# Activations that come turned: centring by an accumulating DMA in place of TensorE transposes

## The chip, the cores and the metric

The kernel runs on one core of a Trainium2 chip. The metric is the device time of one execution in microseconds (us). The engines are named as the profile names them: PE (TensorE, matrix products; PEld is its loading of weights), DVE (VectorE), ACT (ScalarE), POOL (GpSimd) and SP (SyncE). Each works through a queue of its own in order and waits on semaphores for the others. DMAs are issued from the queues of SP, ACT and POOL.

## The reference

The input x has 2048 rows (tokens) of 512 features. Its rows are normalised, and two mixers work on the result: a linear attention with softmax feature maps, and a gated MLP whose gate mixes along the tokens. Both outputs and x are added.

```
xn = (x - mean(x)) / sqrt(var(x) + 1e-5)          # per row
A: q, k, v = xn @ wqkv, in 32 heads of 16
   phi(t)  = [softmax(t @ w_phi), softmax(-(t @ w_phi))]
   o       = phi(q) (phi(k)^T v) / (phi(q) sum_s phi(k) + 1e-6);   A = o @ wo
B: z = gelu(xn @ w_in);  z1, z2 = the halves of z;  z2 = layernorm(z2)
   B = (z1 * (w_sp @ z2 + b_sp)) @ w_out
out = x + A + B
```

All in float32.

## The kernel before

**Tiles.** x is cut into NT = 16 tiles of 128 tokens. A matrix product contracts over the partitions, so each tile is needed turned: features in the partitions, tokens along the row. For precision, every float32 operand is split in two parts (a rounded one, `h`, and the remainder, `l`), and a product is made of three matmuls (`mm3`, lines 55 to 57). ACT rounds (`round_h`, line 47) and DVE takes the remainder (`rest_l`, line 51).

**The first stage** (the part that the change touches) goes over the tiles `s` and, in each, takes the keys' projection of tile s with its softmax features (`proj_k`, `softmax_pair`), prepares tile s + 2 (`centered`), projects queries (`proj_q`, which starts late and catches up), adds the tile's features to a running sum (`add_kv`, by an accumulating DMA of POOL into `zacc`, and at s = 3, 7, 11, 13 and 15 by matmuls into `kvps`), projects the values of tile s + 1 (`proj_v`) and one half of the MLP's input product (`z1_raw`).

**Preparing a tile** (`centered`): `stats` takes mean and variance on DVE (lines 260 and 261); POOL negates the mean (`neg_mean`, line 265) and computes 1/sqrt(var + eps) (`rstd_of`, lines 92 and 93), which is applied later as a scale of ACT; ACT adds the negative mean to the tile (`center`, line 269); PE turns it with four 128x128 transposes into PSUM (`transposed`, line 275, tile `pt`); and `split_x` rounds it (ACT) and takes the remainder (DVE), both reading PSUM, into the tile `xT[s]`, which the projections of this tile read. The loads of x are issued by SP four tiles ahead (`fetch`, line 179), into XB = 5 buffers.

**Buffers.** PSUM gives four buffers of the tag "mm" to the projections of keys, queries and values and to `pt`. In SBUF, 16 slots of the pool `xz` hold the turned tiles `xT`, which stay; until they are all taken, the slots hold staged weights and, from `spare`, the features `er` of the key tiles 2, 3, 4, 5, 8 and 9.

**Order.** The order on each engine comes from a planner, which runs a model of the whole program and takes at each point the instruction of the highest priority (program order) that is ready by its own costs. `tc.issue_after(i)` pins what the block issues on i's engine behind i; `keep` does the same for the first tiles, whose order is written out by hand. Semaphores and the release of buffers are put in by the framework.

**Later stages**: the other half of the MLP's input product (`zps` with `w2`), the token mixing (`g`, matmuls from 281 us to 493 us in the profile below), and the output products (`pout`).

The host passes `x_t` to the kernel in the version before too: for each tile, the features in the partitions, and in row p the values of features p, 128 + p, 256 + p and 384 + p for its 128 tokens. It is not read there.

Of the kernel before, what the change touches and what calls it, by code (L numbers as in the profile page):

```python
# [10 lines left out]
F32 = mybir.dt.float32  # L11
F32R = mybir.dt.float32r
AF = mybir.ActivationFunctionType
ALU = mybir.AluOpType
# [4 lines left out]
P = 128  # L19
S, D, H, DH, FH = 2048, 512, 32, 16, 688  # L20
NT = S // P
ND = D // P
FC = FH // 2
NG = 4
NF = 2 * D
# [3 lines left out]
BL = 32  # L29
EPS_LN = 1e-5  # L30
EPS_DEN = 1e-6
XB = 5
NP = NT // 2
HP, QP = P // 2, P // 4
FP = 3 * P
# [4 lines left out]
def mixer(ctx: ExitStack, tc: tile.TileContext, x, x_t, wv, wqkT, phi_bd, wo, w_in, wst, b_r, w_out, out):  # L40
    nc = tc.nc
    pe, act, dve, pool, sp = nc.tensor, nc.scalar, nc.vector, nc.gpsimd, nc.sync


    def round_h(eng, h, src):
        if eng is act:
            return act.activation(h, src, AF.Copy).ins  # L47
        return eng.tensor_copy(h, src).ins

    def rest_l(l, src, h, eng=None):  # L50
        return (eng or dve).tensor_tensor(l, src, h.bitcast(F32), op=ALU.subtract).ins  # L51
# [18 lines left out]
    def xz_tile(n, dt, name):  # L70
        return xz.tile([P, SL], dt, tag="xz", name=name)[:, :n]

    mid = ctx.enter_context(ExitStack())
    dram = ctx.enter_context(tc.tile_pool(name="dram", bufs=1, space=DRAM))
# [2 lines left out]
    u_d = dram.tile([NT, FU, P], F32, name="u_d")  # L77
    kvT_d = dram.tile([P, D], F32, name="kvT_d")
    zb_d = dram.tile([P, NF], F32, name="zb_d")

    ident = cst.tile([P, P], F32, name="ident")
    make_identity(nc, ident)
# [4 lines left out]
    r_x = cst.tile([P, NT], F32, name="r_x")  # L87

    def rstd_of(mv, r, stats=None):
        if stats is not None:  # L90
            dve.bn_aggr(mv, stats)
        pool.tensor_scalar_add(mv[:, 1:2], mv[:, 1:2], EPS_LN)
        pool.tensor_tensor(r, mv[:, 1:2], mhalf, op=ALU.pow)

    def heads(ap):
        return ap.rearrange("p (h d) -> p h d", d=DH)
# [8 lines left out]
    def bc(ap, n):  # L105
        return ap.unsqueeze(2).to_broadcast([P, n, DH])

    def softmax_pair(pl, src, tag, scale=1.0, ebufs=2, meanwhile=lambda: None, er=None):

        mm = pl.tile([P, 2, H], F32, tag=tag + "mm", bufs=1, name="mm")  # L110
        dve.tensor_reduce(mm[:, 0], heads(src), axis=AX.X, op=ALU.max)
        dve.tensor_reduce(mm[:, 1], heads(src), axis=AX.X, op=ALU.min)
        if er is None:
            er = pl.tile([P, NF + 2 * H], F32, tag=tag + "e", bufs=ebufs, name="e")
        e, r = er[:, :NF], er[:, NF:]
        e2 = e.rearrange("p (h a d) -> p h a d", a=2, d=DH)
        dve.tensor_tensor(e2[:, :, 0], heads(src), bc(mm[:, 0], H), op=ALU.subtract)
        dve.tensor_tensor(e2[:, :, 1], bc(mm[:, 1], H), heads(src), op=ALU.subtract)  # L118
        act.activation(e, e, AF.Exp, scale=scale)  # L119
        meanwhile()  # L120
        sm = pl.tile([P, 2 * H], F32, tag=tag + "sm", bufs=1, name="sm")
        dve.tensor_reduce(sm, heads(e), axis=AX.X, op=ALU.add)  # L122
        dve.reciprocal(r, sm)
        return er
# [34 lines left out]
    mask = w1_pool.tile([P, 2 * P], F32, name="mask")  # L159
# [3 lines left out]
        pool.affine_select(out=mv_, in_=mv_, compare_op=ALU.is_ge, fill=0.0, base=base,  # L163
                           pattern=[[-k * DH, P // DH], [0, 2 * DH]], channel_multiplier=k)
    pool.tensor_tensor(mask[:, :P], mask[:, :P], mask[:, P:], op=ALU.add)
    mask = mask[:, :P]
    ones = w1_pool.tile([P, P], F32, name="ones")
    pool.memset(ones, 1.0)
    zacc = w1_pool.tile([P, NF], F32, name="zacc")
# [2 lines left out]
    with ExitStack() as p0:  # L172
        res = p0.enter_context(left("p0res", 1))
        wk = p0.enter_context(left("p0wk", 2))
        ps = p0.enter_context(psum("p0ps", 4))

        def load_x(s):
            t = wk.tile([P, D], F32, tag="x", bufs=XB, name="xt")
            sp.dma_start(t, x[s * P:(s + 1) * P, :])
            return t  # L180
# [5 lines left out]
        def stage(name, dt=F32):  # L186
            return xz_tile(2 * FH, dt, name).rearrange("p (a b) -> p a b", a=2)
# [6 lines left out]
        bd_t = stage("bd")  # L194
# [50 lines left out]
        xt, v, rounded, ready = {}, {}, [], []  # L245

        def fetch(s):
            if s < NT:
                xt[s] = load_x(s)

        def split_x(src):
            t = xz_tile(2 * D, F32R, "xT").rearrange("p (a b) -> p a b", a=2)
            xT.append(t)
            src = src.rearrange("p a b -> p (a b)")
            rounded.append(round_h(act, t[:, 0], src))
            return rounded[-1], rest_l(t[:, 1], src, t[:, 0])

        def stats(s, keep=lambda **ins: None):
            st6 = wk.tile([P, 6], F32, tag="st6", name="st6")
            dve.bn_stats(st6, xt[s])  # L260
            keep(dve=dve.bn_aggr(mv_x[:, s], st6).ins)

        def neg_mean(s):
            nm = wk.tile([P, 1], F32, tag="nm", name="nm")
            pool.tensor_scalar_mul(nm, mv_x[:, s, 0:1], -1.0)
            return nm

        def center(s, nm):
            return act.activation(xt[s], xt[s], AF.Identity, bias=nm).ins

        def transposed(s):
            xs = xt.pop(s)
            pt = ps.tile([P, ND, P], F32, tag="mm", name="pt")
            for c in range(ND):
                ins = pe.transpose(pt[:, c], xs[:, c * P:(c + 1) * P], ident).ins
            return pt, ins

        def centered(s):
            stats(s)
            nm = neg_mean(s)  # L280
            rstd_of(mv_x[:, s], r_x[:, s:s + 1])
            with tc.issue_after(rounded[s - 2]):
                center(s, nm)
            split_x(transposed(s)[0])

        def keep_v(s, p):
            v[s] = wk.tile([P, D], F32, tag="v", bufs=4, name="v")
            return act.activation(v[s], p, AF.Copy, scale=r_x[:, s:s + 1]).ins
# [5 lines left out]
        spare = {}  # L294

        def proj_k(s):
            er = spare[s].rearrange("p a b -> p (a b)")[:, :NF + 2 * H] if s in spare else None
            return softmax_pair(wk, proj(s, wqk_h[:, 1], wqk_l[:, 1]), "k", r_x[:, s:s + 1], er=er)

        def proj_q(s):  # L300
# [28 lines left out]
        wkT_t = load_rows.raw  # L329
        fetch(2)  # L330
        wqT = load_rows(wqkT[:D])
        wqT_t = load_rows.raw
        fetch(3)
        w1r = [stage("w1row") for _ in range(2)]
# [43 lines left out]
        t = xz_tile(2 * D, F32R, "xT").rearrange("p (a b) -> p a b", a=2)  # L378
# [8 lines left out]
        for cs, pt in zip(halves, pts):  # L387
            src = pt.rearrange("p a b -> p (a b)")
# [8 lines left out]
        p = ps.tile([P, D], F32, tag="mm", name="proj")  # L397
        proj(0, wv_h, wv_l, p, (0, 1, 2))
        keep(pe=proj.last)
        pt = turned(1)  # L400
# [4 lines left out]
        p = ps.tile([P, D], F32, tag="mm", name="proj")  # L405
# [18 lines left out]
        p = ps.tile([P, D], F32, tag="mm", name="proj")  # L424
        proj(0, wqk_h[:, 1], wqk_l[:, 1], p, (0, 1))
        keep(pe=proj.last)
        pt = turned(2)
# [18 lines left out]
        split_x(turned(3))  # L446
        z1_raw(wk, za, 0, 2)
        keep(pe=zproj.last)
        spare.update(zip((2, 3, 4, 5, 8, 9), [bd_t] + wkT_t + wqT_t[:1] + w1r))
        n1, nq = 1, 0  # L450
        for s in range(NT):
            fetch(s + 4)
            er = ek[s] if s < len(ek) else proj_k(s)
            if 1 < s < NT - 2:
                centered(s + 2)
            while nq < (s - 2) * NT // (NT - 3):
                proj_q(nq)
                nq += 1
            add_kv(s, er)
            if s == 0:  # L460
                tiles = fold_tiles(((za, "z"), (ps, "mm")))
                keep(pe=fold(0, wqT, tiles))
                folded(0, tiles)
            elif s == 1:
                proj_v(3)
            elif 2 < s < NT - 1:
                proj_v(s + 1)
            while n1 < s * (NT - LAG) // (NT - 1):
                z1_raw(wk, za, n1, 2)
                n1 += 1  # L470
            if s == 3:
                queue.close()
# [33 lines left out]
    NQ = NT // QC  # L506
    NC = NP * NQ


    SEQ = [(i, q) for i in range(NP) for q in (range(NQ) if i < NP - 1 else (1, 2, 3, 0))]  # L510

# [40 lines left out]
    with ExitStack() as p1:  # L552
# [44 lines left out]
        for s in range(NE):  # L597
            et = load_q(s, tb.tile([P, QW], F32, name="et") if s else tmp1.tile([P, 4, D], F32, tag="zhl", name="et").rearrange("p a b -> p (a b)")[:, :QW])
            tmp = zw.tile([P, 4, FC], F32, tag="z2", bufs=2, name="qtmp").rearrange("p a b -> p (a b)")[:, :NF]
            e, _ = q_fin(et, tmp, zb)  # L600
# [57 lines left out]
    for s in range(NT):  # L658
        p = zproj((kv_ps_p, zc, zbp, za)[s % 4], s, w2, (0, 1) if s % 2 == 0 else (1, 0))
# [7 lines left out]
        for k, q in p:  # L667
            ins = act.activation(z[:, k], q, AF.Gelu_apprx_tanh, scale=r_x[:, s:s + 1]).ins
# [5 lines left out]
        mv = zw.tile([P, 2], F32, tag="mv", bufs=2, name="mv")  # L674
# [61 lines left out]
    def gate(i, cb, z, u, ut, after=None):  # L736
# [10 lines left out]
        def turn():  # L747
# [3 lines left out]
            for b in range(0, P, BL):  # L751
                (pool if i == NP - 2 else sp).dma_start(dst[:, :, b:b + BL], src[b:b + BL].rearrange("p (m b) -> p m b", b=BL))

# [49 lines left out]
    for n in range(NC):  # L803
        i = SEQ[n][0]
        if n % NQ == 1 and i < NP - 1:
            z = load_z1(i)
        products(n, g)
        if n % NQ == NQ - 1 and i < NP - 1:
            c = gt.tile([P, 2, FU], F32, tag="c", name="c")
# [5 lines left out]
        if n + 2 < NC:  # L815
            A[n + 2] = prep_a(n + 2, raw.pop(n + 2))
        if n % NQ == NQ - 1 and i < NP - 1:
            turn = gate(i, cb, z, c, z, prep_a.last)
# [12 lines left out]
        if n == NC - 2:  # L831
            es[0], es[1] = first_q(0), first_q(1)
            t = xz_tile((KF + 1) * P, F32R, "u1")
# [10 lines left out]
    wk = ctx.enter_context(left("cwk", 2))  # L844
# [125 lines left out]
    p, nxt = {}, dict(enumerate(uT))  # L970
# [61 lines left out]
```

## Time and profile before

| | before |
|---|---|
| median of 3 runs (lowest to highest) | 628.2 us (628.04 to 629.95) |
| the profiled execution | 627.78 us |
| its span, first to last instruction | 626.1 us |
| busy PE / DVE / ACT / POOL | 619.1 / 508.8 / 280.7 / 104.8 us |
| mean granted clock of PE | 0.999 |
| moved by DMA | 98.40 MB |

All rows of the prediction come from this one profiled execution. A row of the timeline has start, duration, engine, line of the kernel, operation, output and inputs, shape, and in brackets the idle time of the engine before it with what ended it. A row of groups has the line, engine and operation, the shape, the count, the busy time in all and the mean duration of one in ns, and behind the second bar the idle time before these instructions. Matmuls overlap, so the starts of matmuls say more than their durations. A row of DMA issues ends with the size of one and the median time in us from issue to landing. A row of waits has the total, the count and the longest.

### The profile page before, as it was taken

To read this page: it belongs to the slowest core of one execution; us is meant where nothing else is said; L and a number is where in the kernel's file an instruction comes from. 1 tells how busy PE (TensorE), PEld (TensorE's weight loads), DVE (VectorE), ACT (ScalarE), POOL (GpSimd) and SP (SyncE) were. 2 spreads that over 40 slices of the span, in tenths; PEclk is the share of its full clock that TensorE was granted. 3 is DMA by queue.
4 is the path that set the end of the run, shared out by engine and by line. 5 is a ranking of instruction groups with operands and counts; after the bars stand their busy time and mean duration, and the time that the engine had idled before them with its cause. 6 is when DMAs were issued, how large, how long until landed. Compare 5 with 4: busy or idle time off the path is not lost.

```text
span 626.1 us, 11429 instructions
## 1 busy us (share of the span) xinstructions
PE 619.1 (99%) x4406; PEld 565.3 (90%) x4406; DVE 508.8 (81%) x893; ACT 280.7 (45%) x446; POOL 104.8 (17%) x187
## 2 busy tenths in 40 slices
PE   8999999999999999999999999999999999999996
PEld 7888888888888999999999999999999877788775
DVE  5999998987988398989898897696978899989211
ACT  5653434443333367877434444243445433334331
POOL 4142122111011015442000000000000212211110
PEclk9999999999999999999999999999999999999999
DMA  9445465354336868001454845637367799984722
GB/s 313 164 109 144 121 156 155 88 143 136 104 93 173 274 234 285 2 2 35 147 115 147 193 96 153 136 119 175 88 174 232 224 297 330 320 249 97 180 34 51
DMA packets 87590, 98.40 MB, mean 157 GB/s; under 512 B 46560, under 2 KB 59616, under 8 KB 87296
## 3 DMA queue, kind: packets, MB, share of 16 engines
q1 hardware_dynamic: 75200, 58.12, 32.4%
q0 software_dynamic: 10032, 33.92, 20.7%
q10 hardware_dynamic: 2304, 5.64, 2.4%
q8 instruction: 34, 0.56, 0.4%
q14 instruction: 20, 0.16, 0.1%
HBM read 56.37 MB, written 30.54 MB: 139 GB/s over the span
## 4 chain that ended last, share of the span: by engine, by line
PE 98%; DVE 0%; ACT 0%; POOL 0%; issue 0%; DVEq 0%; POOLq 0%
PE g L57 11%; PE g L56 11%; PE g L55 11%; PE proj L57 7%; PE proj L55 7%; PE proj L56 7%; PE zps L57 6%; PE zps L55 6%; PE zps L56 6%; PE pout L55 5%; PE pout L57 5%; PE pout L56 5%; PE ptq L890 1%; PE po L905 1%; PE kvps L319 1%; PE pout L919 1%
## 5 line engine op out<-in xcount | busy, mean ns | idle before, releaser
L56 PE MATMUL g<-B,A 128*128 128x344 f32 x448 | 143.3, 320 | 0.0
L55 PE MATMUL g<-B,A 128*128 128x344 f32 x448 | 142.8, 319 | 0.0
L57 PE MATMUL g<-B,A 128*128 128x344 f32 x448 | 140.6, 321 | 0.1
L55 PEld LDWEIGHTS g<-B,A 128*128 128x128 f32 x448 | 84.3, 188 | 0.0
L56 PEld LDWEIGHTS g<-B,A 128*128 128x128 f32 x448 | 84.2, 188 | 0.0
L57 PEld LDWEIGHTS g<-B,A 128*128 128x128 f32 x448 | 83.6, 188 | 0.4 <-DVE A L51 0.4
L47 ACT ACTIVATE A<-S 128x512 fp32r<-128x512 f32 x64 | 39.4, 630 | 71.3 <-DVE S L542 51.3
L55 PE MATMUL proj<-wqk_h,xT 128*128 128x512 f32 x128 | 50.6, 395 | 0.0
L57 PE MATMUL proj<-wqk_h,xT 128*128 128x512 f32 x128 | 50.2, 393 | 0.0
L56 PE MATMUL proj<-wqk_l,xT 128*128 128x512 f32 x128 | 49.9, 390 | 0.0
L47 ACT ACTIVATE A<-wf 128x512 fp32r<-128x512 f32 (+1 forms) x64 | 33.2, 521 | 36.3 <-DMA wf<-in_wst 14.3
L119 ACT ACTIVATE e<-e,r_x 128x1024 f32<-128x1024 f32 x26 | 29.9, 1150 | 40.2 <-DVE e L118 39.6
L51 DVE TENSOR_TENSOR A<-S,A 128x512 fp32r<-128x512 f32 x64 | 43.1, 686 | 4.8 <-ACT A L47 4.3
L55 PE MATMUL zps<-w_0h,xT 128*128 128x344 f32 x128 | 41.4, 323 | 0.0
L57 PE MATMUL zps<-w_0h,xT 128*128 128x344 f32 x128 | 41.0, 320 | 0.0
L55 PE MATMUL zps<-w_1h,xT 128*128 128x344 f32 x128 | 40.9, 320 | 0.0
L57 PE MATMUL zps<-w_1h,xT 128*128 128x344 f32 x128 | 40.7, 319 | 0.0
L56 PE MATMUL zps<-w_0l,xT 128*128 128x344 f32 x128 | 40.6, 317 | 0.0
L56 PE MATMUL zps<-w_1l,xT 128*128 128x344 f32 x128 | 40.6, 317 | 0.0
L51 DVE TENSOR_TENSOR A<-wf,A 128x512 fp32r<-128x512 f32 (+1 forms) x64 | 35.0, 549 | 2.6 <-ACT A L47 2.4
L707 POOL DMA_DIRECT2D z1t<-z_d x16 | 8.7, 547 | 165.5 <-DMA u_d<-z1t 98.7
L122 DVE TENSOR_REDUCE sm<-e 128x64 f32<-128x1024 f32 x26 | 31.4, 1207 | 5.1 <-ACT e L119 5.0
(205 smaller groups left out, 1432.7 us busy)
## 6 DMA issues: line engine op xcount, KB each, us to landing
wf<-in_wst SPq DMA_DIRECT2D x64, 256.0 KB, 3.4
e_d<-e POOLq DMA_DIRECT2D x16, 544.0 KB, 4.6
et<-e_d SPq DMA_DIRECT2D x16, 544.0 KB, 6.4
er<-et POOLq DMA_DIRECT2D x12, 512.0 KB, 6.4
z_d<-z1f ACTq DMA_DIRECT2D x16, 344.0 KB, 2.6
z1t<-z_d POOLq DMA_DIRECT2D x16, 344.0 KB, 5.2
zacc<-e POOLq DMA_DIRECT2D x10, 512.0 KB, 4.7
u<-u_d SPq DMA_DIRECT2D x15, 320.0 KB, 5.6
```

Source lines behind the costliest of these rows:

```text
L47: return act.activation(h, src, AF.Copy).ins
L51: return (eng or dve).tensor_tensor(l, src, h.bitcast(F32), op=ALU.subtract).ins
L55: pe.matmul(dst, ah, bh, start=start, stop=False)
L56: pe.matmul(dst, ah, bl, start=False, stop=False)
L57: return pe.matmul(dst, al, bh, start=False, stop=stop).ins
L119: act.activation(e, e, AF.Exp, scale=scale)
L122: dve.tensor_reduce(sm, heads(e), axis=AX.X, op=ALU.add)
L319: i = pe.matmul(kv_acc[k:k + QP, m // 4], vs[:, m * QP:(m + 1) * QP], e[:, m * HP:(m + 1) * HP], start=first and m < 4 and len(ready) == n ...
L707: pool.dma_start(t[:, k, :FH], z1_d[2 * i + k])
L890: pe.transpose(pt[:, a, k].bitcast(F32R), src, ident_r)
L905: lasts[3] = pe.matmul(po[r][c * QP:(c + 1) * QP, k], kvT[rows, m // 2, cols], fs[m // 4][rows, m // 2 % 2], start=True, stop=True).ins
L919: lasts[2] = pe.matmul(p, rt, w, start=False, stop=i == NT - 1 and k == 1).ins
```

## The change

From tile FT = 6 on, x is loaded twice: once as before, for the statistics only, and once turned (`lay_x`, from `x_t`), four tiles ahead of the loop. The mean has to be taken from the turned tile along its rows, where it differs from element to element. For that, `send_mean` puts mean and variance of the 128 tokens into the first two of 32 scratch columns, DVE transposes these in 32x32 blocks, POOL negates the result, and SP stores the negative means to DRAM as a row of 4 x 128 values (the same 128 four times, in pieces of 128 bytes). `center_t` then issues a DMA on POOL that reads this row for all 128 partitions and adds it to the turned tile in SBUF. `split_x` takes its source from that tile. The transposes on PE, their PSUM tile and ACT's centring are gone for tiles 6 to 15.

Statistics for tile s + 4, the accumulating DMA for tile s + 3 and the split of tile s + 2 are issued in round s of the loop. The order is pinned: the statistics behind the last remainder on DVE, the accumulating DMA behind POOL's negation for the next tile, the split behind the key features' last subtraction (DVE) and exponential (ACT). The turned tiles lie in pairs in `xz` slots, from LT = 13 on in the buffers of x. The features `er` of tiles 8 and 9 take `xz` slots of their own, so that the two staged weight tiles are given back early. The scratch columns are the second half of the tile `mask`, which is free by then, cleared once.

```diff
+FT, LT = 6, 13
+    nm_d = dram.tile([NT, ND, P], F32, name="nm_d")
...
-        dve.tensor_tensor(e2[:, :, 1], bc(mm[:, 1], H), heads(src), op=ALU.subtract)
-        act.activation(e, e, AF.Exp, scale=scale)
+        less = dve.tensor_tensor(e2[:, :, 1], bc(mm[:, 1], H), heads(src), op=ALU.subtract).ins
+        softmax_pair.last = less, act.activation(e, e, AF.Exp, scale=scale).ins
...
-    mask = mask[:, :P]
+    mask, scratch = mask[:, :P], mask[:, P:].rearrange("p (a k b) -> p a k b", a=2, k=2)
+    pool.memset(scratch, 0.0)
...
+        def lay_x(s):
+            if s >= LT:
+                xc = wk.tile([P, D], F32, tag="x", bufs=XB, name="xt")
+            elif (s - FT) % 2 == 0:
+                lay_x.pair = xz_tile(2 * D, F32, "xc")
+                xc = lay_x.pair[:, :D]
+            else:
+                xc = lay_x.pair[:, D:]
+            sp.dma_start(xc, x_t[s].rearrange("p c t -> p (c t)"))
+            lay[s] = xc
+
+        def send_mean(s):
+            mv, turn = scratch[:, s % 2, 0], scratch[:, s % 2, 1]
+            st6 = wk.tile([P, 6], F32, tag="st6", name="st6")
+            with tc.issue_after(split_x.last):
+                dve.bn_stats(st6, xt.pop(s))
+            dve.bn_aggr(mv[:, :2], st6)
+            dve.transpose(turn, mv)
+            send_mean.last = pool.tensor_scalar_mul(turn, turn, -1.0).ins
+            sp.dma_start(nm_d[s].rearrange("c (b t) -> b c t", t=BL), turn[0:P:BL].unsqueeze(1).to_broadcast([P // BL, ND, BL]))
+            rstd_of(mv[:, :2], r_x[:, s:s + 1])
+
+        def center_t(s):
+            with tc.issue_after(send_mean.last):
+                pool.dma_start(lay[s], nm_d[s].rearrange("c t -> (c t)").unsqueeze(0).to_broadcast([P, D]), accum_op=ALU.add)
...
-            er = spare[s].rearrange("p a b -> p (a b)")[:, :NF + 2 * H] if s in spare else None
+            er = (spare[s] or stage("er")).rearrange("p a b -> p (a b)")[:, :NF + 2 * H] if s in spare else None
...
-        spare.update(zip((2, 3, 4, 5, 8, 9), [bd_t] + wkT_t + wqT_t[:1] + w1r))
+        spare.update(zip((2, 3, 4, 5, 8, 9), [bd_t] + wkT_t + wqT_t[:1] + [None] * 2))
         n1, nq = 1, 0
         for s in range(NT):
-            fetch(s + 4)
+            if s + 4 < FT:
+                fetch(s + 4)
+            if FT <= s + 6 < NT:
+                fetch(s + 6)
+            if FT <= s + 4 < NT:
+                lay_x(s + 4)
             er = ek[s] if s < len(ek) else proj_k(s)
-            if 1 < s < NT - 2:
+            if 1 < s < FT - 2:
                 centered(s + 2)
+            elif FT - 2 <= s < NT - 2:
+                with tc.issue_after(softmax_pair.last[0]), tc.issue_after(softmax_pair.last[1]):
+                    split_x(lay.pop(s + 2))
+            if FT <= s + 4 < NT:
+                send_mean(s + 4)
+            if FT <= s + 3 < NT:
+                center_t(s + 3)
```

More of the change, by code (lines that the diff above doesn't have):

```diff
@@ L253, in split_x @@
             xT.append(t)
-            src = src.rearrange("p a b -> p (a b)")
             rounded.append(round_h(act, t[:, 0], src))
-            return rounded[-1], rest_l(t[:, 1], src, t[:, 0])
+            split_x.last = rest_l(t[:, 1], src, t[:, 0])
+            return rounded[-1], split_x.last
         def stats(s, keep=lambda **ins: None):
@@ L275, in transposed @@
                 ins = pe.transpose(pt[:, c], xs[:, c * P:(c + 1) * P], ident).ins
-            return pt, ins
+            return pt.rearrange("p a b -> p (a b)"), ins
         def centered(s):
@@ L284, in centered @@
             split_x(transposed(s)[0])
+        lay = {}
+        def lay_x(s):
[21 more added lines that the diff above has]
+                pool.dma_start(lay[s], nm_d[s].rearrange("c t -> (c t)").unsqueeze(0).to_broadcast([P, D]), accum_op=ALU.add)
         def keep_v(s, p):
```

## The prediction

> **What bounds the kernel now.** I read the page first: busy shares, then the chain that ended last.
>
> ```profile
> PE 619.1 (99%) x4406; PEld 565.3 (90%) x4406; DVE 508.8 (81%) x893; ACT 280.7 (45%) x446; POOL 104.8 (17%) x187
> ...
> PE 98%; DVE 0%; ACT 0%; POOL 0%; issue 0%; DVEq 0%; POOLq 0%
> ```
>
> TensorE (PE) is busy 99% of the span, and 98% of the chain is PE's own work, one instruction behind the other. What leaves PE's queue shortens the program, as long as nobody else becomes late. Shares are averages, so the second view is the busy time by stretch: the start, the tiles in which the queries catch up, the later tiles, the end of the first stage.
>
> ```profile
> core 0: us, PE busy (x) PEld busy (x) DVE busy (x) ACT busy (x) POOL busy (x), PEclk, DMA share, GB/s
> 12.00:40.00 28.00, 28.00 (x374) 24.42 (x374) 25.34 (x44) 16.89 (x27) 8.66 (x22) 1.00 0.50 167
> 40.00:88.80 48.80, 48.80 (x366) 42.13 (x365) 47.32 (x74) 20.47 (x27) 11.55 (x24) 1.00 0.53 137
> 88.80:166.00 77.20, 77.20 (x623) 66.53 (x623) 68.14 (x100) 30.74 (x39) 12.95 (x22) 1.00 0.44 125
> 166.00:200.00 34.00, 34.00 (x234) 29.83 (x233) 29.22 (x43) 12.04 (x16) 3.66 (x7) 1.00 0.48 133
> ```
>
> PE never idles here, at a granted clock of 1.00. VectorE (DVE) is the neighbour to watch: 47.32 of 48.80 us between 40 and 88.8, but 68.14 of 77.20 after. ScalarE (ACT) and GpSimd (POOL) are mostly under half, the DMA engines about half.
>
> **What PE loses.** Tiles 6 to 15 need no transposes on PE: ten groups of four. A matmul's duration is no price for them, because matmuls overlap; what counts is how far a group pushes the starts behind it. The third view is PE's timeline around one group.
>
> ```profile
> 88.08 0.40 PE L57 MATMUL proj<-wqk_h,xT 128*128 128x512 f32 x1
> 88.31 0.60 PE L275 MATMUL pt<-ident,xt 128*128 128x128 f32 x4
> 88.67 0.48 PE L55 MATMUL proj<-wqk_h,xT 128*128 128x512 f32 x1
> 88.98 0.39 PE L56 MATMUL proj<-wqk_l,xT 128*128 128x512 f32 x1
> 89.22 0.40 PE L57 MATMUL proj<-wqk_h,xT 128*128 128x512 f32 x1
> 89.45 0.39 PE L55 MATMUL proj<-wqk_h,xT 128*128 128x512 f32 x1
> ```
>
> The undisturbed step is 0.23 us (89.22 to 89.45). From the matmul at 88.08 to the third one behind the group, at 89.22, pass 1.14 us, where three steps would take 0.69. The group costs 0.45 us of PE; ten groups, 4.5 us.
>
> [...]
>
> **The other engines, edit by edit.** Rows of the first 200 us, and for the DVE transpose the nearest one, of a later stage.
>
> ```profile
> L269 ACT ACTIVATE xt<-xt,nm 128x512 f32<-128x512 f32 x15 | 10.6, 713 | 0.5 <-POOL mv_x L92 0.5
> ...
> L51 DVE TENSOR_TENSOR xT<-pt,xT 128x512 fp32r<-128x512 f32 x15 | 10.1, 672 | 1.9 <-ACT xT L47 1.9
> ...
> L51 DVE TENSOR_TENSOR wv_l<-wrow,wv_h 128x512 fp32r<-128x512 f32 x4 | 2.7, 688 | 0.1
> ...
> L260 DVE BATCH_NORM_STATS2 st<-xt 128x6 f32<-128x512 f32 x16 | 10.7, 680 | 6.7 <-DMA xt<-in_x 6.7
> ...
> L261 DVE BATCH_NORM_AGGREGATE mv_x<-st 128x2 f32<-128x6 f32 x16 | 2.7, 172 | 0.2
> ...
> L749 DVE STREAM_TRANSPOSE z1t<-c 128x1472 f32<-128x1472 f32 x7 | 11.9, 1704 | 0.0
> ...
> L93 POOL TENSOR_TENSOR r_x<-mv_x,mhalf 128x1 f32<-128x1 f32 x16 | 9.6, 601 | 1.0
> ...
> L308 POOL DMA_DIRECT2D zacc<-e x10 | 9.1, 909 | 60.9 <-DVE e L307 30.1 <-DVE e L123 27.4 <-ACT wqk_h L47 2.3
> L92 POOL TENSOR_SCALAR mv_x<-mv_x 128x1 f32<-128x1 f32 x16 | 4.5, 282 | 14.7 <-DVE mv_x L261 13.8
> L265 POOL TENSOR_SCALAR nm<-mv_x 128x1 f32<-128x1 f32 x15 | 3.5, 234 | 34.6 <-DVE mv_x L261 24.2 <-ACT xt L269 9.9
> ```
>
> ACT loses ten centrings, 7.1 us; it is not the bound, so nothing for the time. DVE keeps statistics and remainder (read from SBUF 688 ns against 672 from PSUM: 0.2 us over ten) and gains ten 128x32 transposes. The row of 128x1472 scaled down gives 0.04 us as a lower end; as an upper end I take a whole 0.68 us pass; I take 0.17, the row of the likewise small aggregation. DVE: +1.9 us (0.6 to 7). POOL gains the issue of ten accumulating DMAs, 9 us at 909 ns, on an engine that is idle most of the time; nothing for the time, as long as the DMA leaves in time (the new chain, below). The clearing of the scratch columns is one fill of 128x128 on POOL at the start, beside the first weights' splitting.
>
> ```profile
> 1.22 0.21 POOL L168 MEMSET ones<- 128x128 f32 x1
> ```
>
> It counts as nothing; uncovered, it would be 0.2 us.
>
> ```profile
> xt<-in_x SPq DMA_DIRECT2D x16, 256.0 KB, 3.9
> ...
> zacc<-e POOLq DMA_DIRECT2D x10, 512.0 KB, 4.7
> ...
> out<-xr POOLq DMA_DIRECT2D x15, 256.0 KB, 5.8
> ...
> u_d<-z1t POOLq DMA_DIRECT2D x4, 184.0 KB, 7.5
> ```
>
> These are DMA issues with their size and the median time to landing. The DMA queue of SyncE (SP) gains ten loads of 256 KB and ten stores of means; the accumulates move another 256 KB each. That is 5.2 MB over some 110 us, 47 GB/s beside 125 to 137, with the DMA engines about half free. SP's stores wait for POOL, and the next loads queue behind them; these loads are issued one tile (laid-out x) or two (statistics) ahead of use, against 3.9 us of landing, so a delay of one tile's head is covered.
>
> **The one new chain.** The order pins form a loop: remainder of tile t on DVE, then the statistics of t+2, aggregation and transpose, POOL's negation and two rstd instructions (which stand ahead of it in the queue), the accumulating DMA of t+1, its landing, ACT's rounding of t+1, its remainder.
>
> ```profile
> 56.67 0.68 DVE L51 TENSOR_TENSOR xT<-pt,xT 128x512 fp32r<-128x512 f32 x1
> 57.27 0.68 DVE L117 TENSOR_TENSOR wrow<-proj,mm 128x512 f32<-128x512 f32 x1
> 57.86 0.68 DVE L118 TENSOR_TENSOR wrow<-mm,proj 128x512 f32<-128x512 f32 x1
> ...
> 158.03 0.68 DVE L51 TENSOR_TENSOR xT<-pt,xT 128x512 fp32r<-128x512 f32 x1
> ...
> 167.44 0.63 DVE L51 TENSOR_TENSOR xT<-pt,xT 128x512 fp32r<-128x512 f32 x1
> ```
>
> ```profile
> 166.06 0.60 ACT L47 ACTIVATE xT<-pt 128x512 fp32r<-128x512 f32 x1 [1.86 <-PE pt L275]
> ```
>
> Without the landing it takes 0.68 + 0.68 + 0.17 + 0.17 on DVE, 0.23 + 0.28 + 0.60 on POOL, and 1.38 from rounding to remainder (166.06 to 167.44): 4.2 us. The landing is unknown: no row shows an accumulate into SBUF from one 2 KB row of DRAM for all 128 partitions. Between 3.9 (a plain load of this size) and 7.5 (POOL's slowest) I take 4.7, the accumulate of twice the size. The loop then needs 8.9 us (8.1 to 11.7). Before, remainders followed each other every (167.44 - 56.67) / 9 = 12.3 us, the closest pair 9.4 us. So it fits, with 0.5 us in the tightest pair. The stored means have a whole tile to arrive.
>
> What lies behind a wait there: ACT's rounding blocks the exponentials behind it, then DVE's sums. PE is covered by earlier work.
>
> ```profile
> 62.74 0.39 PE L55 MATMUL proj<-wqk_h,xT 128*128 128x512 f32 x1
> ...
> 169.09 0.39 PE L55 MATMUL proj<-wv_h,xT 128*128 128x512 f32 x1
> ```
>
> The turned tile whose remainder ran at 158.03 is first used at 169.09, 10.4 us after its end. For PSUM I paired projections with their readers, for four "mm" buffers: without the transposes' share of them the closest case behind 50 us is the projection at 62.74, whose buffer was free at 58.54 (end of the subtraction at 57.86), 4.2 us before. So DVE may fall that far behind.
>
> Will it? Four groups lie between 40 and 88.8: PE needs 48.8 - 1.8 = 47.0 us there, DVE 47.32 + five transposes (0.9) = 48.2. DVE falls behind by 1.2 us, or 2.7 with its present idle 1.5. That is under 4.2, and after 88.8 DVE has 9.1 us of idle time, less 2.7 that PE saves there and 0.9 for transposes, so it catches up. I cost it at nothing.
>
> The second stage's first loads wait for the last projection, so they move along with PE.
>
> ```profile
> SPq L489 <- PE proj L57: 91.2, 1, 91.2
> ```
>
> Sum: 627.78 (the profiled execution) - 4.5 = 623.3. The median is 0.4 above that execution, so 623.7.
>
> **Rivals.** First, DVE becomes the bound between 40 and 88.8: the cushion doesn't hold, because the order of the queues differs or POOL and DVE disturb each other. The trace has a hint of the latter.
>
> ```profile
> 38.20 1.10 POOL L92 TENSOR_SCALAR mv_x<-mv_x 128x1 f32<-128x1 f32 x1 [0.88 <-DVE mv_x L261]
> ```
>
> ```profile
> 38.03 1.19 DVE L307 TENSOR_TENSOR e<-e 128x1024 f32<-128x1024 f32 x1
> ```
>
> POOL's instruction, 0.28 us on average, took 1.10 beside a DVE operation with both inputs in SBUF and ended with it. The remainder now has both inputs in SBUF as well. [...]
>
> For DVE's side I take at most POOL's 0.60 us per tile, in six tiles 3.6. Then the 1.8 us of the four groups are lost, and the stretch takes 48.2 to 49.7 us of DVE plus up to 3.6: with the 2.7 us of the six later groups, a gain of 3.3 at best and a loss of 1.8 at worst; 627.4 in the middle. A transpose at the upper end of its price leads here too.
>
> Second, and on the other side: the accumulate lands late. 128 rows all read the same 2 KB, which no row prices. The loop would then set the pace: from 12.3 us on (a landing of 8.1) the kernel is no faster than before, and at a landing of 9 us the loop takes 13.2, nine times 0.9 more: 636. Against it: no median landing among POOL's DMAs quoted is over 7.5.
>
> Third, the gain moves elsewhere: all queues are planned ahead as a whole, so later stages may be ordered differently, by some 2 us either way.
>
> **How the numbers follow.** Forecast (PE's 4.5 us, all else covered) 0.62; DVE bound early 0.17; late accumulate 0.13; re-ordered elsewhere 0.08. A measurement here tells some 0.3%, 1.9 us, from no change. Faster: 0.62, 0.06 of the second case and 0.03 of the last: 0.71. Same: 0.10 of the second and 0.04 of the last: 0.14. Slower: 0.01 of each of these two and the late accumulate: 0.15. The forecast's own range is 622 to 626 (the upper end with a landing of 7.5, where a few close pairs wait some 2 us). The range with the second case and the re-ordering is 621 to 629.5; it leaves out the late accumulate and little else.
>
> **What would show it.** Right: 20 matmuls in the transposes of "pt" at line 275's place instead of 60, the stretch up to the last first-stage matmul 4.5 us shorter, PE without idle, accumulates landing in 4 to 6 us. Wrong: PE waiting for a DVE release between 40 and 90 us (first rival), ACT's rounding waiting several us for a DMA in most tiles (second), or a first stage shorter by 4.5 us and a later one longer (third).

## The result, and the profile after

The changed kernel takes 625.18 us (median of 6 runs, 624.49 to 625.68) against 629.03 us of the kernel before on the same chip: a ratio of 0.9939, with a 95% interval of 0.9926 to 0.9952. Measured twice more, it gave 0.9956 [0.9939, 0.9974] and 0.9943 [0.9925, 0.9962]. So it is faster by some 0.5%, 2.8 to 3.8 us by these ratios, inside the predicted range. It is 1.5 us above the predicted 623.7; 0.8 us of that is the kernel before itself, 629.03 us here against the 628.2 from which the prediction started. The profiled execution took 625.34 us, its span 623.6.

The page of the changed kernel, first the busy times, then the chain that ended last:

```profile
PE 615.1 (99%) x4366; PEld 561.5 (90%) x4366; DVE 508.3 (82%) x903; ACT 272.8 (44%) x436; POOL 113.7 (18%) x198
...
DMA packets 90671, 103.67 MB, mean 166 GB/s; under 512 B 47080, under 2 KB 60136, under 8 KB 90376
...
PE 85%; DMA 6%; DVE 4%; issue 3%; POOL 1%; ACT 1%; DVEq 0%; POOLq 0%
```

PE still is the bound, with 4.0 us less of busy time. But the chain is no longer PE's alone: 15% of the span it runs through other engines, DMAs and issues, where before it was PE for 98%. The busy time by stretch, columns as before:

```profile
40.00:88.80 48.80, 48.80 (x360) 42.35 (x359) 44.55 (x73) 18.07 (x24) 13.63 (x26) 1.00 0.70 172
88.80:166.00 77.20, 75.98 (x604) 65.03 (x603) 72.54 (x118) 27.19 (x35) 23.82 (x40) 1.00 0.65 163
166.00:200.00 34.00, 34.00 (x298) 30.28 (x297) 30.84 (x45) 12.88 (x17) 4.86 (x7) 1.00 0.55 153
```

DVE, the neighbour to watch, had 44.55 us of work between 40 and 88.8 (47.32 before): it didn't become the bound; part of its work came later (72.54 against 68.14 in the next stretch). Between 88.8 and 166, PE idles 1.22 us. The waits, the whole span (total, count, longest), name what it waited for:

```profile
ACT xT L48 <- DMA xc<-nm_d: 17.0, 7, 4.0
...
DVE xT L52 <- ACT xT L48: 7.7, 7, 2.9
...
ACT xT L48 <- DMA xt<-nm_d: 3.1, 2, 2.4
...
PE proj L56 <- ACT xT L48: 1.2, 1, 1.2
```

ACT's rounding waits for the accumulating DMA in nine of the ten turned tiles, 20.1 us in all; DVE's remainder waits behind it; and once, at 126, PE waits for such a late rounding.

To follow the time through the program I use four marks on PE: the start of the last value projection (the end of the first stage, as the prediction named it), the first and the last start of the token mixing's `g`, and the span. The first mark is read from rows like this one of before and this one of after.

```profile
183.45 0.39 PE L57 MATMUL proj<-wv_h,xT 128*128 128x512 f32 x1
```

```profile
180.16 0.39 PE L58 MATMUL proj<-wv_h,xT 128*128 128x512 f32 x1
```

| kernel (one profiled execution each) | last value projection | first `g` | last `g` | span |
|---|---|---|---|---|
| before | 183.45 | 281.05 | 493.11 | 626.1 |
| changed | 180.16 | 277.98 | 490.01 | 623.6 |
| changed, second (e5) | 180.02 | 278.58 | 490.63 | 623.4 |
| changed, third (e12) | 179.55 | 278.15 | 490.20 | 623.7 |
| before, tiles left unturned (e7) | 178.43 | 276.03 | 488.08 | 624.4 |
| accumulate first (e1) | 178.44 | 275.56 | 487.60 | 621.2 |
| accumulate first, again (e10) | 178.40 | 277.12 | 489.16 | 623.2 |
| accumulate first, transposes back (e6) | 183.48 | 281.08 | 493.11 | 626.8 |
| transposes back (e3) | 188.53 | 286.70 | 498.76 | 632.0 |
| mean in one piece (e8) | 177.90 | 278.17 | 490.83 | 624.1 |
| no accumulate (e2) | 178.68 | 276.65 | 488.69 | 622.0 |
| accumulate twice (e9) | 213.33 | 307.61 | 520.54 | 654.2 |
| accumulate first, from tile 5 (e11) | 177.53 | 275.82 | 487.87 | 621.1 |

The first stage became 3.3 to 3.9 us shorter, not 4.5. (Work is ordered alike around the first mark in all of these but two: in e8 64 short matmuls into `kvps`, 1.1 us, stand behind it instead of ahead and four of `zps`, 0.6 us, ahead instead of behind; in e9 more of `zps` is ahead of it. The later marks of e1 come 1.6 us earlier than those of its repetition e10; the last section says why they aren't typical.)

### The profile page after: what moved, and what is told of

Its sections match the earlier page's. It is cut to its first block, busy times and chain, and to the rows that moved or that the text cites. A ratio compares the mean times of both kernels' runs of the same rounds, so it can differ in the third digit from the quotient of the medians.

```text
span 623.6 us, 11439 instructions
## 1 busy us (share of the span) xinstructions
PE 615.1 (99%) x4366; PEld 561.5 (90%) x4366; DVE 508.3 (82%) x903; ACT 272.8 (44%) x436; POOL 113.7 (18%) x198
## 4 chain that ended last, share of the span: by engine, by line
PE 85%; DMA 6%; DVE 4%; issue 3%; POOL 1%; ACT 1%; DVEq 0%; POOLq 0%
PE g L58 11%; PE g L57 10%; PE g L56 10%; PE zps L58 6%; PE zps L56 6%; PE zps L57 6%; PE pout L56 5%; PE pout L58 5%; PE pout L57 5%; DMA xc<-nm_d 5%; PE proj L56 4%; PE proj L57 4%; PE proj L58 4%; PE ptq L936 1%; PE po L951 1%
```

## The experiments

Two questions: is a group of transposes worth what the prediction put on it, and what took back the rest? My theory on the second was the loop of accumulating DMAs, which the prediction had called fitting; the rival was that the order elsewhere gave it back.

### The first term: the transposes

**e7**: the kernel before, with the transposes of tiles 6 to 15 simply left out; the centred tile is split as it is.

```diff
-            split_x(transposed(s)[0])
+            if s >= 6:
+                split_x(xt.pop(s).rearrange("p (a b) -> p a b", b=P))
+            else:
+                split_x(transposed(s)[0])
```

> The kernel before without the transposes of tiles 6 to 15: these tiles are split as they are, from SBUF, so their projections are of unturned data. No mean is sent and nothing is accumulated. The prediction's first term alone: 10 groups of 0.45 us, 4.5 us less than before, ratio 0.993. If before also lost time to waits that PE's modelled busy time hides, it is more: 5.5 us (0.991), as the early accumulate showed against before in the first stage.

Measured: 624.15 us, ratio 0.9928 [0.9912, 0.9945], so 4.5 us less than before (3.5 to 5.5), and a first stage shorter by 5.02 us. The term stands alone here, without a transpose on DVE, a mean in DRAM or an accumulate (it includes what the transposes take of the PSUM buffers), and the time is the predicted one. (By the span the gain looks like 1.7 us: this profiled execution lost 3.3 us behind the last `g`. PE waited 1.91 us there, from 516 on, and then ran at a granted clock of 0.50 from 519 to 521. The marks up to the last `g` show 5.0.)

**e3**: the changed kernel, with four transposes put back on PE for each turned tile, into a PSUM tile that nobody reads.

```diff
+                idle = ps.tile([P, ND, P], F32, tag="mm", name="idle")
+                for c in range(ND):
+                    pe.transpose(idle[:, c], ident, ident)
```

> As after the change, but PE does four 128x128 transposes of the identity into an unread PSUM tile for each of tiles 6 to 15, where the turned tile is split: only PE's time and PSUM buffers are as before. Theory (the gain is PE's queue alone, 0.44 us for four): span 3.2 to 4.4 us longer than after the change, 626.8 to 628.0, ratio to before 0.999 to 1.001 (the lower end if the 1.2 us wait then disappears under PE's work). Rival (the gain comes from ACT's ten centrings or the PSUM reads that are gone): span near 623.6, ratio 0.994.

Measured: 634.24 us, ratio 1.0085 [1.0062, 1.0107]. That is some 9 us above the changed kernel, nearly twice what ten groups are worth, and slower than before: the expectation missed. The waits of e3:

```profile
ACT xT L48 <- DMA xc<-nm_d: 21.6, 7, 3.5
...
DVE xT L52 <- ACT xT L48: 16.3, 11, 3.1
...
PE zps L56 <- ACT z1f L151: 1.6, 2, 1.4
...
PE kvps L353 <- DVE e L341: 1.4, 1, 1.4
...
PE proj L56 <- ACT v L322: 1.2, 1, 1.2
```

PE now waits 4.2 us for ACT and DVE. ACT waits for the accumulates, and DVE for ACT, longer than in the changed kernel (21.6 against 17.0, 16.3 against 7.7), and the remainders of the turned tiles follow each other every 13.1 us (63.43 to 181.45) instead of 12.2. So a work of PE's own that pushes nothing but PE can't be priced in this kernel without regard to the loop. To part the two, **e6** does the same in the kernel of e1 (below), where the loop is loose:

> The accumulate one round earlier, and four transposes of the identity into an unread PSUM tile for each of tiles 6 to 15. With the loop cut, only PE's transposes differ from the kernel with the early accumulate (span 621.2 us). Theory (a group costs PE 0.44 to 0.45 us, and the 10 us that the same groups cost in the changed kernel came from the loop, which they made longer): span 625.6 to 626.2 us, ratio to before 0.998 to 1.000. Rival (the groups themselves cost more, through PSUM buffers or weight loads): span 629 us or more.

Measured: 628.11 us, ratio 0.9986 [0.9972, 0.9999], and no wait of ACT for an accumulate. Its first stage ends 5.04 and 5.08 us after that of the two runs of its base (e1, e10). With e7 that is twice the same answer: ten groups, 5.0 us of the first stage, 0.50 us each; the 3.4 us that e3 lost beyond them (188.53 - 180.16 - 5.0) hang on the loop. In the time the answer is less sharp: by the ratios e6 is 1.9 to 3.2 us above its base (0.9956 and 0.9935), e7 4.5 us below before.

### The second term: the loop

**e1**: in each round, the accumulate for tile s + 3 is issued ahead of the statistics for tile s + 4, so it no longer stands behind the next tile's negation on POOL.

```diff
-            if FT <= s + 4 < NT:
-                send_mean(s + 4)
             if FT <= s + 3 < NT:
                 center_t(s + 3)
+            if FT <= s + 4 < NT:
+                send_mean(s + 4)
```

> The accumulating DMA of tile s+3 is issued ahead of the statistics of tile s+4, so that it is pinned only behind its own mean: one round of the loop earlier. Theory (the loop remainder - statistics - negation - accumulate - rounding paces tiles 7 to 11 and costs PE 1.2 us at the values' projection of tile 11): ACT's waits for the accumulate (17.0 us in seven tiles after the change) go to near 0, PE's 1.2 us wait goes, span 1.2 us shorter than after the change: 622.4 us, ratio to before 0.992. Rival (the wait comes from PE's own order, or the DMAs are late whatever the order): waits and span as after the change, 623.6 us, ratio 0.994.

Measured: 624.35 us, ratio 0.9935 [0.9914, 0.9956]. The waits went as the theory said: ACT waits for no accumulate and PE for no rounding any more. The time does not decide: the theory's 0.992 and the rival's 0.994 both lie in the interval. In the waits of the first 200 us of e1 the one that is left is on POOL, which has the time:

```profile
POOL xc L318 <- DMA nm_d<-mask: 11.3, 4, 4.1
```

**e2** leaves the accumulate out:

```diff
-            if FT <= s + 3 < NT:
-                center_t(s + 3)
```

> Leaves the accumulating DMA out, so that tiles 6 to 15 are not centred; the statistics, the stores of means and the turned loads stay. Theory: PE saves 4.4 us against before and nothing waits: span 622.3 us, ratio to before 0.992. Rival (the extra loads and the DVE transposes cost too): span stays near 623.6 although no rounding waits for an accumulate.

Measured: 623.73 us, ratio 0.9919 [0.9897, 0.9941], as the theory said. Its first stage ends at 178.68, near e1's at 178.44. So 178.4 to 178.7 is where the first stage ends if nothing waits for the loop, and against e1 and e10 the loop costs the changed kernel 1.1 to 1.8 us there.

**e8** asks which part of the loop was long. It pins the query projections and the feature sums of the round behind the transpose of the mean, so that statistics, aggregation and transpose follow each other closely on DVE.

```diff
-            dve.transpose(turn, mv)
+            send_mean.turned = dve.transpose(turn, mv).ins
...
+            with ExitStack() as behind:
+                if FT <= s + 4 < NT:
+                    behind.enter_context(tc.issue_after(send_mean.turned))
+                ...
```

> The changed kernel with DVE's aggregation and transpose pinned ahead of the queries' and the running sum's work of the same round, so that they directly follow the statistics. Theory (the prediction's loop sum was wrong in DVE's term: 0.34 us by the durations, 2 to 5 us in the queue, because other passes stand between): the transpose starts 2 us after the statistics' start in place of 3 to 6, the loop gets 2 to 4 us shorter, ACT's waits for the accumulate fall below 8 us in all, PE's wait goes; ratio 0.992. Rival (landing, not DVE's order, sets the loop): waits stay at 17 us.

The same part of DVE's timeline, first in the changed kernel, then in e8:

```profile
62.35 0.69 DVE L52 TENSOR_TENSOR xT<-xc,xT 128x512 fp32r<-128x512 f32 x1
62.95 0.69 DVE L308 BATCH_NORM_STATS2 st<-xt 128x6 f32<-128x512 f32 x1
63.55 0.54 DVE L125 RECIPROCAL wrow<-sm 128x64 f32<-128x64 f32 x1
64.01 1.16 DVE L124 TENSOR_REDUCE sm<-e 128x64 f32<-128x1024 f32 x1
65.08 0.17 DVE L309 BATCH_NORM_AGGREGATE mask<-st 128x2 f32<-128x6 f32 x1
65.17 1.20 DVE L341 TENSOR_TENSOR wrow<-wrow 128x1024 f32<-128x1024 f32 x1
66.28 0.55 DVE L125 RECIPROCAL e<-sm 128x64 f32<-128x64 f32 x1
66.74 0.15 DVE L310 STREAM_TRANSPOSE mask<-mask 128x32 f32<-128x32 f32 x1
...
77.35 0.69 DVE L52 TENSOR_TENSOR xT<-xc,xT 128x512 fp32r<-128x512 f32 x1 [2.91 <-ACT xT L48]
```

```profile
61.40 0.68 DVE L52 TENSOR_TENSOR xT<-xc,xT 128x512 fp32r<-128x512 f32 x1
62.00 0.69 DVE L308 BATCH_NORM_STATS2 st<-xt 128x6 f32<-128x512 f32 x1
62.60 0.53 DVE L125 RECIPROCAL wrow<-sm 128x64 f32<-128x64 f32 x1
63.05 0.12 DVE L309 BATCH_NORM_AGGREGATE mask<-st 128x2 f32<-128x6 f32 x1
63.21 0.21 DVE L310 STREAM_TRANSPOSE mask<-mask 128x32 f32<-128x32 f32 x1
...
72.02 0.68 DVE L52 TENSOR_TENSOR xT<-xc,xT 128x512 fp32r<-128x512 f32 x1
```

From the remainder to the transpose pass 4.39 us in the changed kernel, because four feature passes (0.54, 1.16, 1.20, 0.55) stand between its steps; in e8 it is 1.81 us, with one pass left between. ACT's waits for accumulates are gone, and with them PE's. So DVE's order was the term that made the loop long, and the rival recorded for this run (the landing sets the loop, the waits stay at 17 us) is out. The first stage gains by it what it gains in e1: the first query projection behind all work that changed places starts at 182.46, against 184.07 in the changed kernel and 182.35 in e1, 1.6 us earlier. But the time did not follow: 626.10 us, ratio 0.9960 [0.9944, 0.9976], not the expected 0.992. The 1.6 us are given back by the first `g` (278.17 against 277.98). The waits of e8 between 200 and 230 show how:

```profile
DVE w_0l L52 <- DMA z_d<-z1f: 10.2, 1, 10.2
ACT z1f L151 <- DMA wst__2226<-in_w_in: 5.3, 1, 5.3
...
PEld pz L618 <- ACT zhl L48: 0.8, 2, 0.4
...
PEld pz L619 <- DVE zhl L52: 0.4, 1, 0.4
PEld zps L56 <- ACT w_0h L48: 0.4, 1, 0.4
PEld zps L57 <- DVE w_0l L52: 0.4, 1, 0.4
```

PE's weight loads wait 1.2 us for ACT and DVE to split the operand `zhl` of the matmuls `pz` (0.2 us in the changed kernel), and 0.8 us for the second stage's weights `w_0`, which DVE and ACT split behind waits for DMAs. Together that is 2.0 us, about the loss; no run takes these waits out to show it. So for the time of e8 the rival of this section, the order elsewhere, is right.

**e4** tests another explanation of the loop's length: that an accumulate lands late because all 128 partitions read the same 2 KB. It adds 128 different rows instead.

```diff
-                pool.dma_start(lay[s], nm_d[s].rearrange("c t -> (c t)").unsqueeze(0).to_broadcast([P, D]), accum_op=ALU.add)
+                pool.dma_start(lay[s], x_t[s].rearrange("p c t -> p (c t)"), accum_op=ALU.add)
```

> The accumulating DMA takes its addend from 128 different rows of DRAM (the turned tile itself) in place of one row of 2 KB for all partitions; the sums are other numbers, the queues are the same. If the single row makes the landing slow (the second rival of the prediction), the landing falls from 5.2 us (4.0 to 7.7) to the 4 us of a plain load. If not, it stays at 5 us or gets longer.

The DMA issues of e4, and below them those of the changed kernel (size, median us to landing):

```profile
xc<-in_x_t POOLq DMA_DIRECT2D x7, 256.0 KB, 5.1
...
xt<-in_x_t POOLq DMA_DIRECT2D x3, 256.0 KB, 4.3
```

```profile
xc<-nm_d POOLq DMA_DIRECT2D x7, 256.0 KB, 5.2
...
xt<-nm_d POOLq DMA_DIRECT2D x3, 256.0 KB, 4.0
```

The landing is the same, ACT waits 16.8 us in seven instead of 17.0, and the single run took 625.63 us. The repeated source row costs nothing that shows here.

### How near the second rival was

**e9** issues every accumulate twice, one behind the other.

```diff
             if FT <= s + 3 < NT:
                 center_t(s + 3)
+                center_t(s + 3)
```

> The changed kernel with each tile's accumulating DMA issued twice, so the mean is subtracted twice (the output is another one). The two accumulate into the same tile, so the second lands behind the first: the time from POOL's issue to ACT's rounding grows from about 6 to 10 or 12 us, by the 4 to 5.2 us that one landing takes. Loop theory (the accumulate stands in a closed loop with DVE's remainder, and the loop of the changed kernel already runs at 12 to 15 us a tile): the remainders follow each other every 16 to 19 us, PE waits for roundings through tiles 7 to 15, and the time is 625 + eight or nine tiles x 4 to 5 = 657 to 670 us. Rival (the mean leaves early enough that ten microseconds of lead take up a second landing): the remainders stay at 12 to 13 us, and the time is 625 to 630.

Measured: 656.42 us, ratio 1.0437 [1.0414, 1.0459]. Remainders of the turned tiles ran from 66.11 to 201.34, one each (201.34 - 66.11) / 9 = 15.0 us; in the changed kernel (62.35 to 171.73) it is 12.2. That is under the expected 16 to 19, and the time is just under the loop theory's 657 to 670; the rival's 625 to 630 is out. So the loop sets the pace as soon as one landing is added. (In this run the second accumulate was issued only when the first had landed, so it also held up POOL's queue, 20.5 us in five tiles; the run doesn't part the two.) PE's waits for roundings (19.8 us) are not all: behind each of the three longest (7.13, 5.12 and 4.67 us) PE also ran slower for a while.

```profile
86.11 0.80 PE L56 MATMUL proj<-wv_h,xT 128*128 128x512 f32 x1 [7.13 <-ACT xT L48]
```

```profile
86.00:90.00 4.00, 3.89 (x13) 3.70 (x13) 3.91 (x8) 1.46 (x3) 0.00 (x0) 0.50 0.84 259
90.00:94.00 4.00, 4.00 (x19) 3.50 (x19) 4.00 (x7) 2.14 (x4) 1.55 (x4) 0.91 0.02 4
```

Behind the 7.13 us the granted clock was 0.50 in the 4 us from 86 on, and PE's steps at 344 columns were 0.29 us, against 0.15 at 77 to 79 us. Behind the 5.12 and the 4.67 us the steps at 512 columns were 0.43 us, against 0.23, for 3.5 and 5.7 us. The length of the wait alone doesn't tell it here: behind the 1.91 us of e7 the granted clock was 0.50 as well, while behind one of 2.48 us in e9 it stayed at 1.00 (steps of 0.23 us from 181.87 on). What sets the clock these runs don't show.

### Is the loop worth anything in the time?

Three kernels, measured side by side. **e12** is the changed kernel; **e10** is e1 once more; **e11** is e1 with x turned from the fifth tile on.

```diff
-FT, LT = 6, 13
+FT, LT = 4, 13
...
-            if s + 4 < FT:
-                fetch(s + 4)
-            if FT <= s + 6 < NT:
+            for k in range(4, 7) if s == 0 else ():
+                fetch(k)
+            if 0 < s < NT - 6:
                 fetch(s + 6)
```

> The changed kernel once more, beside the two others of this call: 625.2 to 626.1 us, PE's wait of 1.2 us for the rounding of tile 11 at 126 again.

> The accumulate of tile s+3 issued ahead of the negated mean of tile s+4, once more, beside the changed kernel in the same call. Loop theory: PE's 1.2 us wait at 126 goes, and with it 1 to 1.5 us of the time: 624.3 against 625.5. Rival (what the first stage gains is given back by another order later): the same time as the changed kernel within 0.5 us.

> The accumulate ahead of the mean, and x turned from the fifth tile on instead of the seventh, so two groups of four transposes fewer on PE (12 instead of 20 transposes). By the price of a group (0.45 to 0.55 us) 0.9 to 1.1 us less than the same order from the seventh tile: 623.3. Rival (DVE, at 24.4 to 25.3 busy of 28 us between 12 and 40 us, or the first landings at the start become the bound): no faster, or 1 to 3 us slower, with PE waiting for a rounding or a remainder between 20 and 60 us.

An earlier repeat of the changed kernel, **e5**, had been expected so:

> The changed kernel itself, beside the others of this series on one chip: ratio to before 0.993 to 0.995, ACT's waits for the accumulate 17 us in seven tiles and PE's wait of about 1 us at a values' projection, as in its first profile.

Measured: e5 626.07 us, ratio 0.9956 [0.9939, 0.9974]; e12 625.42 us, 0.9943 [0.9925, 0.9962]; e10 625.15 us, 0.9956 [0.9935, 0.9977]; e11 623.11 us, 0.9916 [0.9900, 0.9931]. The ratio of e5 is a little above what was expected for it. PE's wait at 126 came in every profiled execution of the changed kernel (1.22, 1.22 and 0.82 us) and in neither that of e1 nor that of e10, whose first stages end 1.1 to 1.8 us earlier. Yet the medians of e10 and e12 are 0.3 us apart: here too the rival was nearer. The marks show where it went in this pair: 1.15 us ahead at the last value projection, 1.0 at the last `g`, 0.5 in the span, with a wait of 0.97 us of PE for DVE at 517 in e10 alone. Whether e1 is faster than the changed kernel by up to a microsecond stays open.

e11 came out at the forecast 623.3, in part by luck: two groups fewer made the first stage 0.87 us shorter than e10's, as forecast (0.9 to 1.1), but the time is 2.0 us below e10's, and why the rest came is open. PE waits for no rounding and no remainder. It is the fastest kernel here; its interval lies well below 1, and its upper end overlaps the interval of the changed kernel beside it a little (0.9931 against 0.9925).

## Why the prediction was right, and what in it was wrong

**PE as the bound, ten groups at 0.45 us.** Right in kind, a little small in size: 5.0 us of the first stage in e7 and in e6, 0.50 us a group, and 4.5 us in the time of e7. The reading of the one group was right for all ten: in the trace of before each pushes the third matmul behind it by 0.44 to 0.46 us. But the push still grows behind that: for the eight groups that can be followed for some twenty matmuls, it ends at 0.46 to 0.53 us (against steps of 0.227 us for 512 columns and 0.154 for 344). Three matmuls were too few to read the price from. The 5.0 us over 40 transposes are 0.125 us each. The row of groups shows what is left: `pt` with 20 matmuls.

```profile
L278 PE MATMUL pt<-ident,xt 128*128 128x128 f32 x20 | 3.0, 272 | 0.0
...
L310 DVE STREAM_TRANSPOSE mask<-mask 128x32 f32<-128x32 f32 x10 | 1.9, 191 | 0.0
```

**The other engines' terms.** DVE's transposes: 1.9 us in ten, where 0.17 each had been taken from the small aggregation (0.19 measured); the upper end, a whole pass, was far off. POOL: 9 us forecast, 8.9 measured (104.8 to 113.7). ACT: 7.1 forecast, 7.9 measured. DMA: 5.2 MB forecast, 5.27 measured. None of them stood ahead of PE by its size; the place of DVE's transposes in the queue is another matter (the loop, below).

**First rival, DVE as the bound.** It did not come: DVE had 2.8 us less to do between 40 and 88.8 than before, in part because work came later, and the cushion there was not needed. The up to 3.6 us that this rival put on DVE's side, beside POOL, were the author's estimate, and no run shows them: the ten remainders with both inputs in SBUF took 0.69 us each (692 ns on average in seven, 687 in three), those of 128x512 from PSUM in the same execution 685 ns.

**The loop: the step that failed.** The prediction summed the loop to 8.9 us and called it fitting. The longest turn of it in the changed kernel, from the remainder at 62.35 to the next at 77.35, took 15.0 us; the eight full turns (62.35 to 160.95) took 12.3 us on average, each with ACT waiting for the accumulate. The rows of DVE stand above; these are POOL's, and ACT's at the end:

```profile
66.90 0.88 POOL L342 DMA_DIRECT2D zacc<-wrow  x1 [5.52 <-DVE mask L310]
67.46 0.88 POOL L336 DMA_DIRECT2D e_d<-e  x1
68.41 0.32 POOL L311 TENSOR_SCALAR mask<-mask 128x32 f32<-128x32 f32 x1
68.81 0.22 POOL L94 TENSOR_SCALAR mask<-mask 128x1 f32<-128x1 f32 x1
68.98 0.92 POOL L318 DMA_DIRECT2D xc<-nm_d  x1
```

```profile
76.69 0.63 ACT L48 ACTIVATE xT<-xc 128x512 fp32r<-128x512 f32 x1 [3.81 <-DMA xc<-nm_d]
```

| part of the turn | predicted | longest turn | mean of eight (least to most) |
|---|---|---|---|
| remainder to transpose (DVE) | 0.68 + 0.68 + 0.17 = 1.53 | 66.74 - 62.35 = 4.39 | 5.09 (4.00 to 6.39) |
| transpose to accumulate (DVE, POOL) | 0.17 + 1.11 = 1.28 | 68.98 - 66.74 = 2.24 | 1.16 (0.86 to 2.24) |
| landing, to ACT's rounding | 4.7 (3.9 to 7.5) | 76.69 - 68.98 = 7.71 | 5.11 (4.01 to 7.71) |
| rounding to remainder | 1.38 | 77.35 - 76.69 = 0.66 | 0.97 (0.66 to 3.11) |
| sum | 8.9 | 15.0 | 12.33 |

The term that failed in every turn is DVE's: it added durations of instructions as if each followed its predecessor at once, and the planner put feature passes between them (3.45 us in four, in the turn above). The slot of an instruction in a busy engine's queue is a cost of its own, and the prediction had no term for it: 1.53 us became 5.1. The other terms were right on average. On POOL, DMA issues of the running sums or the features stood in between in two of the eight turns, and only one of the two rstd instructions stood ahead of the accumulate. The landing of 4.7 was a fair mean, though one landing lies above its range. The four longest landings (5.2 to 7.7 us, tile 6's among them) belong to accumulates issued 1.5 to 3.1 us behind a DMA of 512 KB of running sums from POOL's queue; the five others on which ACT waited had none of these in the 5 us before them and took 4.0 to 5.0 us. Whether that DMA is the cause was not tested. The consequences were named properly (ACT's rounding waits for a DMA in most tiles), but as the sign of the second rival, with 0.13; they came in nine tiles of ten while the mean spacing stayed at 12.2 us. So it was neither the forecast nor the rival: the loop ran at its edge and took 1.1 to 1.8 us in the first stage.

**"PE is covered by earlier work"**, a turned tile ready 10.4 us before its use. The cover held in all places but one: at 126 PE came to the values' projection of tile 11 before ACT had rounded it. By the starts it lost 127.68 - 126.07 - 0.23 = 1.4 us there, most of what the loop took in this execution.

```profile
126.07 0.39 PE L58 MATMUL proj<-wqk_h,xT 128*128 128x512 f32 x1
127.68 0.50 PE L56 MATMUL proj<-wv_h,xT 128*128 128x512 f32 x1 [1.22 <-ACT xT L48]
```

**Third rival, the order elsewhere.** Small in the change itself (3.3 us ahead at the first mark, 3.1 at the first and last `g`, 2.5 in the span), and decisive in e8, which gave back 2 us.

**The sum.** Forecast 4.5 us, measured 2.8 to 3.8 in the time. For the first stage the account closes: 5.0 us from PE, less 1.1 to 1.8 for the loop, leave the 3.3 to 3.9 us seen there. Two errors of opposite sign, 0.5 us too little for the groups and nothing for the loop, cancelled in part; that the time fell so near the forecast is in part luck. For the time the loop's share is not shown: e1 and e10, where it costs nothing, took ratios of 0.9935 and 0.9956, no faster beyond the noise than the changed kernel's 0.9939 to 0.9956.

## What to carry to other kernels

When a change closes a loop over several engines, add for each step the place that it gets in that engine's queue, not only its duration; here a step of three short instructions on DVE took 5.1 us on average instead of 1.5, behind passes of other work. Look for the pin that closes the loop: issuing the accumulate ahead of the next tile's mean opened it, though without a gain in the time that is clear of the noise. And follow a gain through marks along the program: a first stage shorter by 1 to 2 us was worth less or nothing in the end in e8 and e10.

## What the runs showed of the hardware

Two profiled executions of the same kernel (e1, then e10) were equal up to the last value projection (178.44 and 178.40) and 1.6 us apart at the first `g`, with PE fully busy at a granted clock of 1.00 in both:

```profile
250.00:270.00 20.00, 20.00 (x132) 20.00 (x131) 17.94 (x37) 17.17 (x27) 8.81 (x16) 1.00 0.01 1
```

```profile
250.00:270.00 20.00, 20.00 (x128) 20.00 (x128) 17.95 (x38) 17.34 (x26) 8.48 (x17) 1.00 0.01 1
```

In the same 20 us PE started 132 matmuls in the one and 128 in the other, so a step of 0.152 us against 0.156; the starts themselves show it, and not only the counts. I had expected equal steps at an equal clock; what makes the difference stays open. The other kernels' traces start 128 or 129 there (e9, which runs later, in the 20 us from 264 on), so the first profile of e1 is the exception, and its marks from the first `g` on stand 1.6 us early. Spans of single executions of one kernel thus differ by 2 us (621.2 and 623.2) for reasons that no edit made.
